# Mamba-2 SSD and an ELU feed-forward on one core: the last pair's second layer by 12-bit words instead of Strassen products

## The chip, the core and the metric

The kernel runs on one core of a Trainium2 chip. Its time is device microseconds of that core for one launch. The engines are named as in the profile: PE is TensorE (matmuls), PEld its weight loads, DVE is VectorE, ACT is ScalarE, POOL is GpSimd, SP is SyncE, which issues most transfers.

## The reference

```python
# x [4, 8, 768, 32], a [4, 8, 768], B and C [4, 8, 768, 16]: a chunked scan
y[:, :, sl] = y_intra + y_inter                      # per batch and head, chunks of 32
state = decay_full * state + sum(Bx)
...
x = y.transpose(0, 2, 1, 3).reshape(3072, 256)       # tokens by (head, dim)
h = x @ w_in                                         # [3072, 256] @ [256, 2048]
g = where(h > 0, h, exp(min(h, 0)) - 1)              # ELU
return g @ w_out                                     # [3072, 2048] @ [2048, 256], float32
```

Inputs and output are float32. The two layers of the feed-forward are the bulk of the work of TensorE.

## The kernel before

**Tiles.** The 3072 tokens are 12 blocks of 256 tokens; two blocks make a pair, named by its first block: n = 0, 2, 4, 6, 8, 10 (`NP` is 12). d_ff = 2048 is 16 blocks of 128, numbered m (`MC` is 16). `g_of[n, m]` holds the ELU output of one m: 128 features by two blocks by 256 tokens.

**Order.** The schedule is written out by hand (`tc.manual_schedule()`): each engine runs its instructions in the order of the source, and waits only by semaphore. From pair 4 on there is one stage per pair n, in the loop `for n in range(4, NP, 2)`: 16 steps k. A step computes one m of the first layer of pair n (`l1_words`), and lets the generator `second(n - 2)` go on by three or four pieces (`l2s`), so that the second layer of the pair before is woven in. In the stages of pairs 4 to 8 the scan of the next pair's tokens is woven in too; in that of pair 10, "the last stage" in the prediction, there is none. After the loop the last pair's second layer runs alone: `second(10, True)`.

**First layer by words** (`l1_words`, L779 to L801). An F32R matmul goes through TensorE in one pass, but keeps fewer bits than float32. So each operand is split into a high and a low word of 12 bits, and a product is three F32R passes: high by high and low by low into the PSUM bank `ps_h`, a pass over the sums into `ps_w`. A step's three passes are six matmuls of 128x512 (L788). Behind them comes a ring over two engines: ACT copies `ps_w` to `e` times 4096 (L796); DVE joins `e` with `ps_h` (L799); ACT makes Relu and Exp (L805, L806, `begin_end`); one step later, ahead of the next L799, DVE makes g from both (L813, `end_words`). For even m POOL then takes a difference inside g (L848, `sub`), which the second layer needs.

**Second layer by Strassen** (`second`, L871 to L960). For a pair, 2x2 blocks of g and of w_out are multiplied with 7 products rather than 8: seven rounds r over a `chunk` of four m-pairs, twice (`half`), with 8 float32 products of 128x128 per round (L907). A float32 product is two matmul records in the trace. The sums of g blocks (`sum_t1`, `sum_t2`, and in-place differences) are made by POOL, sums of weight blocks were made ahead (`a_out`, `s_out`: s1 lies in place in `w_out`), results are added up by DVE (L885 and others) with two copies by ACT.

**PSUM.** `p_a` has seven banks in rotation (tag "a"): `ps_h`, `ps_w` and every second round of `second` take the next one, and wait until the instruction that read its former content is done. `p_o` has one bank; the other rounds take that.

**SBUF.** Tiles come from pools by tag, with `bufs` buffers in rotation. Tag "w64" holds first raw weights, then the weight sums, then `k_words` (words of w_in); "w_in" holds w_in and its low words. By the last stage, the scan's tiles ("bct", "ctm", "xr", "bc", "M", "ec", "b", "L", "yT") are free.

**End.** The last `second` writes its output by four transfers (two of them 64 KB, on ACT's and SP's queues), issued as its parts are complete (L893 to L899, L947).

Of the kernel before, what the change touches and what calls it, by code (L numbers as in the profile page):

```python
# [17 lines left out]
P = 128  # L18
# [14 lines left out]
def kernel(  # L33
# [139 lines left out]
    def w_load(i, parts=1):  # L173
        if i < len(pieces):
            w_raw[i] = conv.tile(
                [P, parts, 2, 2 * CW // parts], U32, tag="w64", name="w64", bufs=W_AHEAD)
# [538 lines left out]
        nc.gpsimd.dma_start(out=out[:, rows], in_=in_[:, rows], accum_op=ALU.add)  # L715

    def weight_sums():
        return [conv.tile([P, MC // 2, P], F32, tag="w64", name="w_sum", bufs=W_AHEAD)
                for _ in range(3)]

    w_parts = w_out.rearrange("p (i k) (r c) -> p k r i c", k=2, c=P)
# [10 lines left out]
    def words_of_w(i):  # L732

        w = pieces[i][0]
        k_words[i] = conv.tile(
            [P, 2, KC, CW], F32R, tag="w64", name="w_words", bufs=W_AHEAD)
        nc.scalar.activation(k_words[i][:, 0], w, ACT.Copy, scale=NEAR)
        nc.vector.scalar_tensor_tensor(
            out=k_words[i][:, 1], in0=k_words[i][:, 0].bitcast(F32), scalar=1.0 / WORD - 1.0,
            in1=w, op0=ALU.mult, op1=ALU.add)  # L740
# [27 lines left out]
    def both_of_y(n):  # L768
# [6 lines left out]
                in1=y[:, k], op0=ALU.mult, op1=ALU.add)  # L775
        y_words[n] = y1, y0, both

    def l1_words(n, m, between=None):

        cols = slice(m % 2 * P, (m % 2 + 1) * P)  # L780
        w, w0 = k_words[m // 2]
        w1, both_w, w0 = w[:, 0, :, cols], w[:, 1, :, cols], w0[:, :, cols]
        y1, y0, both_y = y_words[n]
        high, both = psum([P, 2 * BLK], "ps_h"), psum([P, 2 * BLK], "ps_w")
        passes = [(high, w1, y1), (high, w0, y0), (both, both_w, both_y)]
        for ps, lhs, rhs in passes if m == (8 if n == 2 else 0) or m == 15 else passes[2:] + passes[:2]:
            for k in range(KC):
                nc.tensor.matmul(  # L788
                    out=ps, lhsT=lhs[:, k], rhs=rhs[:, k], start=k == 0 and lhs is not w0,
                    stop=k == KC - 1 and lhs is not w1)  # L790
# [5 lines left out]
        nc.scalar.activation(e, both, ACT.Copy, scale=WORD)  # L796
        if late:
            end_words()
        nc.vector.scalar_tensor_tensor(  # L799
            out=high, in0=high, scalar=WORD - 1.0, in1=e, op0=ALU.mult, op1=ALU.add)  # L800
        late.append((n, m, high, e))  # L801
# [66 lines left out]

    c_of = {}

    def second(n, last=False):  # L871
# [5 lines left out]
        s2, s3, s4 = s_out  # L877
        for half in range(2):
# [3 lines left out]
            chunk = range(4 * half, 4 * half + 4)  # L882

            def add(out, in0, in1, eng=nc.vector):
                eng.tensor_tensor(out=out, in0=in0, in1=in1, op=ALU.add)  # L885

            for r, a in enumerate((a11, a12, s1, s2, s3, a22, s4)):
                if last and half and r == 6:
                    store(n, 0)
                    for ts, queue in enumerate((nc.scalar, nc.sync)):  # L890
                        ps = psum([P, P], "ps_o")
                        for i in chunk:
                            nc.tensor.matmul(  # L893
                                out=ps, lhsT=quarters(n, i)[3][:, ts * P:(ts + 1) * P],
                                rhs=a[:, i], start=(i == chunk[0]), stop=(i == chunk[-1]))
                        nc.vector.tensor_tensor(
                            out=c12[:, ts], in0=ps, in1=c12[:, ts], op=ALU.add)
                        r0 = row_of(n + 1) + ts * P
                        queue.dma_start(out=out[r0:r0 + P, 0:P], in_=c12[:, ts])  # L899
                    return  # L900
                pool, tag = (p_a, "a") if (7 * half + r) % 2 else (p_o, "o")
                ps = pool.tile([P, 2, P], F32, tag=tag, name="ps_o")
                for i in chunk:
                    b11, b21, b12, b22 = quarters(n, i)
                    b = (b11, b21, b12, t2_of[n, i], b11, b21, b22)[r]
                    for ts in range(2):
                        nc.tensor.matmul(  # L907
                            out=ps[:, ts], lhsT=b[:, ts * P:(ts + 1) * P], rhs=a[:, i],
                            start=(i == chunk[0] and ts == 0), stop=(i == chunk[-1]),
                            skip_group_check=True)  # L910
                    if i < chunk[-1]:
                        yield
                if r == 0:
                    if half:
                        add(p5, ps, c22)
                        add(c21, ps, c21)
                        add(c11, ps, c11)
                    else:
                        nc.scalar.copy(out=p1, in_=ps)
                    for i in chunk:  # L920
                        b11 = quarters(n, i)[0]
                        sub(b11, t2_of[n, i], b11)
                elif r == 1:
                    add(c11, ps, c11 if half else p1)
                    for i in chunk:
                        b21 = quarters(n, i)[1]
                        sub(b21, b21, t2_of[n, i])
                elif r == 2:
                    add(p5, ps, p5 if half else p1)
                elif r == 3:  # L930
                    add(p5, ps, p5)
                    if half:
                        add(c12, c12, p5, nc.gpsimd)
                        add(c21, ps, c21)
                    else:
                        add(u, ps, p1)
                elif r == 4:
                    if half:
                        add(c21, ps, c21)
                    else:  # L940
                        add(u, ps, u)
                    add(c22, ps, p5)
                    if not half:
                        nc.scalar.copy(out=c12, in_=ps)  # L944
                    if last and half:
                        r0 = row_of(n + 1)
                        nc.sync.dma_start(  # L947
                            out=out[r0:r0 + BLK, P:2 * P].rearrange("(t p) c -> p t c", p=P),
                            in_=c22)
                    if not half:  # L950
                        sum_t2(n, 1)
                    elif n + 2 < NP:
                        sum_t2(n + 2, 0)
# [6 lines left out]
                yield  # L960

    def store(n, at):
        r0 = row_of(n + at)
# [346 lines left out]
    for n in range(4, NP, 2):  # L1310
# [37 lines left out]
        if m:  # L1348
            l2s(4)
            both_of_y(m)  # L1350
        end_words()
# [37 lines left out]
```

## Time and profile before

| what | us |
|---|---|
| median of the runs | 347.59 |
| lowest run | 346.96 |
| the profiled execution | 347.65 |
| its span, first to last instruction | 345.9 |
| last stage (16 steps), from the span's start | 270.42 to 317.49 |
| last pair's second layer alone | 317.49 to 342.66 |
| drain | 342.66 to 345.90 |

The span is shorter than the time because the launch has work around the first and last instruction. A busy time is a sum over instructions, so a share says how full an engine is, not that it is what the others wait for. Matmuls are pipelined: a record of 275 ns can be followed by the next one 112 ns later, so prices of matmuls are taken from start to start, in the chain of work that ended last. In the rows of groups the numbers are minimum/median/maximum in ns; in the rows of the timeline they are start, duration, engine, line, operation, output<-input, shape, and in brackets the idle time before and what ended it.

### The profile page before, as it was taken

To read this page: it belongs to the slowest core of one execution; us is meant where nothing else is said; L and a number is where in the kernel's file an instruction comes from. 1 tells how busy PE (TensorE), PEld (TensorE's weight loads), DVE (VectorE), ACT (ScalarE), POOL (GpSimd) and SP (SyncE) were. 2 spreads that over 40 slices of the span, in tenths; PEclk is the share of its full clock that TensorE was granted. 3 is DMA by queue.
4 is the path that set the end of the run, shared out by engine and by line. 5 is a ranking of instruction groups with operands and counts; after the bars stand their busy time and mean duration, and the time that the engine had idled before them with its cause. 6 is when DMAs were issued, how large, how long until landed. Compare 5 with 4: busy or idle time off the path is not lost.

```text
span 345.9 us, 9861 instructions
## 1 busy us (share of the span) xinstructions
PE 338.7 (98%) x3878; PEld 297.4 (86%) x3878; DVE 253.3 (73%) x504; ACT 238.1 (69%) x541; POOL 215.3 (62%) x321
## 2 busy tenths in 40 slices
PE   8989999999999999999999999999999999999996
PEld 4669888888788898889899888999988999999996
DVE  4898988879898778866788676878676766665222
ACT  5688989599759898657699457699457566565000
POOL 5553553559989699964396664296754264455760
PEclk9999999999999999999999999999999999999999
DMA  8888988470797961070511170410000100001001
GB/s 145 228 231 165 326 178 236 87 140 30 107 151 112 139 108 31 10 162 2 124 45 32 17 153 5 116 22 3 2 0 4 63 0 3 0 0 63 2 1 62
DMA packets 76902, 28.58 MB, mean 83 GB/s; under 512 B 57848, under 2 KB 71736, under 8 KB 76856
## 3 DMA queue, kind: packets, MB, share of 16 engines
q1 hardware_dynamic: 70360, 25.60, 32.2%
q0 software_dynamic: 4176, 2.10, 5.4%
q8 instruction: 30, 0.49, 0.6%
q10 hardware_dynamic: 2320, 0.26, 0.5%
q14 instruction: 16, 0.13, 0.1%
HBM read 22.51 MB, written 3.34 MB: 75 GB/s over the span
## 4 chain that ended last, share of the span: by engine, by line
PE 92%; SPq 2%; DMA 2%; DVE 1%; ACT 1%; issue 1%; POOL 0%; POOLq 0%; ACTq 0%
PE ps_o L907 36%; PE ps_h L788 19%; PE ps_h L671 11%; PE ps_w L788 10%; PE ps_o L832 8%; PE ps_y L638 3%; DMA w<-in_moe_w_in_dram 2%; PE ps_g L545 2%; PE ps_y L620 2%; PE ps_st L575 1%; SPq L179 1%; PE ps_o L893 1%; SPq L132 0%; POOL w_in L252 0%; SPq L116 0%
## 5 line engine op out<-in xcount | busy, mean ns | idle before, releaser
L907 PEld LDWEIGHTS ps_o<-w_out,g 128*128 128x128 f32 x640 | 78.6, 192 | 3.4
L907 PE MATMUL ps_o<-w_out,g 128*128 128x128 f32 x640 | 80.3, 276 | 0.0
L805 ACT ACTIVATE e<-ps_h 128x512 f32<-128x512 f32 x72 | 43.0, 597 | 50.2 <-DVE ps_h L799 50.1
L813 DVE SCALAR_TENSOR_TENSOR g<-e,ps_h 128x512 f32<-128x512 f32 x72 | 49.4, 686 | 34.1 <-ACT e L806 33.7
L848 POOL TENSOR_TENSOR g<-g 128x256 f32<-128x256 f32 x36 | 28.0, 777 | 56.2 <-DVE g L813 56.0
L799 DVE SCALAR_TENSOR_TENSOR ps_h<-ps_h,e 128x512 f32<-128x512 f32 x72 | 50.1, 695 | 12.5 <-ACT e L796 9.7
L788 PE MATMUL ps_w<-y_both,w_words 128*128 128x512 f32 x144 | 51.1, 435 | 0.0
L796 ACT ACTIVATE e<-ps_w 128x512 f32<-128x512 f32 x72 | 42.2, 587 | 12.9 <-PE ps_w L788 12.8
L671 PE MATMUL ps_h<-yT,w_in 128*128 128x256 f32 (+1 forms) x208 | 45.2, 368 | 2.3 <-POOL w_in L252 2.2
L806 ACT ACTIVATE e<-e 128x512 f32<-128x512 f32 x72 | 45.5, 632 | 2.3
L788 PE MATMUL ps_h<-y,w_words 128*128 128x512 f32 x144 | 46.1, 402 | 0.0
L788 PE MATMUL ps_h<-y,w 128*128 128x512 f32 x144 | 44.7, 392 | 0.0
L671 PEld LDWEIGHTS ps_h<-yT,w_in 128*128 128x128 f32 x208 | 36.4, 190 | 8.3 <-POOL w_in L252 3.7
L525 ACT ACTIVATE L<-L,ncum 128x64 f32<-128x64 f32 x160 | 42.2, 336 | 0.2
L907 PE MATMUL ps_o<-w_sum,g 128*128 128x128 f32 x304 | 38.4, 275 | 0.0
L907 PEld LDWEIGHTS ps_o<-w_sum,g 128*128 128x128 f32 x304 | 37.0, 192 | 1.2 <-ACT c_sum L944 0.2
L530 POOL TENSOR_SCALAR_AFFINE_SELECT L<-L 64x512 f32<-64x512 f32 x40 | 30.0, 749 | 9.1 <-ACT L L525 7.7
L788 PEld LDWEIGHTS ps_h<-y,w 128*128 128x128 f32 x144 | 27.1, 188 | 6.5 <-POOL w L848 0.2
L848 POOL TENSOR_TENSOR g<-t,g 128x256 f32<-128x256 f32 x40 | 28.0, 730 | 5.9 <-PE ps_o L907 5.7
L788 PEld LDWEIGHTS ps_h<-y,w_words 128*128 128x128 f32 x144 | 26.4, 188 | 5.7 <-issue 0.4
L832 PE MATMUL ps_o<-w_out,g 128*128 128x256 f32 x128 | 31.0, 384 | 0.0
L848 POOL TENSOR_TENSOR t<-g 128x256 f32<-128x256 f32 x40 | 28.6, 746 | 0.2
(131 smaller groups left out, 535.1 us busy)
## 6 DMA issues: line engine op xcount, KB each, us to landing
L<-flat SPq DMA_DIRECT2D x20, 256.0 KB
w<-in_moe_w_out_dram SPq DMA_DIRECT2D x8, 512.0 KB
w<-in_moe_w_in_dram SPq DMA_DIRECT2D x7, 512.0 KB
xr<-in_x_dram SPq DMA_DIRECT2D x24, 128.0 KB
out_dram<-c_sum SPq DMA_DIRECT2D x9, 256.0 KB
bc<-in_B_dram SPq DMA_DIRECT2D x24, 64.0 KB
w_sum<-w_out POOLq DMA_DIRECT2D x3, 512.0 KB, 8.9
bc<-in_C_dram SPq DMA_DIRECT2D x22, 64.0 KB
```

The costliest lines, as they stand in the source:

```text
L525: nc.scalar.activation(L[:, h, u], L[:, h, u], ACT.Exp, bias=ncum[:, u, row:row + 1])
L530: nc.gpsimd.affine_select(out=part, in_=part, pattern=[[0, 4], [0, 2], [1, Q]], compare_op=ALU.is_ge, fill=0.0, base=0, channel_multiplier=-1)
L671: nc.tensor.matmul(out=ps[:, j, toks], lhsT=w_in[i][:, k, j * P:(j + 1) * P], rhs=yT[n // 2][:, k, n % 2].rearrange("p u i -> p (u i)")[:, ...
L788: nc.tensor.matmul(out=ps, lhsT=lhs[:, k], rhs=rhs[:, k], start=k == 0 and lhs is not w0, stop=k == KC - 1 and lhs is not w1)
L796: nc.scalar.activation(e, both, ACT.Copy, scale=WORD)
L799: nc.vector.scalar_tensor_tensor(out=high, in0=high, scalar=WORD - 1.0, in1=e, op0=ALU.mult, op1=ALU.add)
L805: nc.scalar.activation(e, high, ACT.Relu, scale=-1.0)
L806: nc.scalar.activation(e, e, ACT.Exp, scale=-1.0)
L813: nc.vector.scalar_tensor_tensor(out=g_of[n, m].rearrange("p b i -> p (b i)"), in0=e, scalar=1.0, in1=h, op0=ALU.subtract, op1=ALU.max)
L832: nc.tensor.matmul(out=o_of[n][:, ts], lhsT=g_of[n, j][:, m % 2, ts * P:(ts + 1) * P], rhs=w_out[:, m], start=(m == 0 and ts == 0), stop=( ...
L848: nc.gpsimd.tensor_tensor(out=out, in0=in0, in1=in1, op=ALU.subtract)
L907: nc.tensor.matmul(out=ps[:, ts], lhsT=b[:, ts * P:(ts + 1) * P], rhs=a[:, i], start=(i == chunk[0] and ts == 0), stop=(i == chunk[-1]), s ...
```

## The change

The last pair's second layer is made by words too, as in the first layer: each g and each w_out block is split in three (a high word, a sum word for the pass over sums, a low word), and each product of 128 tokens by 128 features by 256 columns is three F32R matmuls. There are four output tiles of 128 tokens, 16 m and three kinds: 192 matmuls of 128x256. Kind 1 goes to the second half of a tile's bank, kinds 0 and 2 to the first; ACT copies the one and DVE joins both at the end. Three tiles lie in `p_a`, the fourth in `p_o`.

The words are spread: in the last stage ACT makes high words of g (`high_of_g`) in steps 2, 3, 4, 6, 8, 12 and 14 and high words of w_out (`high_of_out`) in steps 5, 7, 9 and 11; DVE makes the other words of g (`rest_of_g`) and the sum word of w_out, POOL its low word (`rest_of_out`), a step later. The others follow in `second_words`, in 14 groups, up to seven groups ahead of their matmuls. POOL restores the weight block that held a sum (`given_back`) in steps 4 and 12. Words of w_out lie in the scan's free tiles (`HOMES`), words of g in the free buffers of "w64" and "w_in".

The order of m is exchanged for pairs 8 and 10: 8 to 15, then 0 to 7. `second(8)` accordingly begins with the second half. For pair 10 the differences that POOL made in g for Strassen are gone (the condition `n + 2 < NP`), and so are the last pair's sums. The buffers of "w64" are split into 8 and 3 ("s64"), by which every tile keeps the place in rotation that it had. `end_words` for the last m moves from the loop's end to the second group of the new part. In the last two m the four tiles are finished one after the other, each with its ACT copy, its DVE join and a transfer of 128 KB from SP.

```diff
+    def ends_of(n):
+        return (8, 7) if n >= NP - 4 else (8, 15) if n == 2 else (0, 15)
...
-        if m % 2 == 0 and (n, m) != (2, 14):
+        if m % 2 == 0 and (n, m) != (2, 14) and n + 2 < NP:
             sub(g_of[n, m][:, 1], g_of[n, m][:, 1], g_of[n, m][:, 0])
...
+    def given_back(rows):
+        sub(a_out[2][:, rows], a_out[2][:, rows], a_out[3][:, rows])
...
+    def high_of_out(at):
...
+        for part, rows in parts_of(v[0], p):
+            nc.scalar.activation(part, w_out[:, rows], ACT.Copy, scale=NEAR)
...
+    def rest_of_out(at):
...
+        for part, rows in parts_of(v_of[p][1], p):
...
+            nc.vector.scalar_tensor_tensor(
+                out=part, in0=high.bitcast(F32), scalar=1.0 / WORD - 1.0, in1=w_out[:, rows],
+                op0=ALU.mult, op1=ALU.add)
+        for part, rows in parts_of(v_of[p][2], p):
...
+            sub(part, w_out[:, rows], high.bitcast(F32))
...
+    def high_of_g(n, m):
...
+        nc.scalar.activation(tiles[0], g_of[n, m], ACT.Copy, scale=NEAR / WORD)
...
+    def rest_of_g(n, m, which=(1, 2)):
+        for k in which:
+            nc.vector.scalar_tensor_tensor(
+                out=h_of[m][k], in0=h_of[m][0].bitcast(F32), scalar=(1.0 - WORD, WORD)[k - 1],
+                in1=g_of[n, m], op0=ALU.mult, op1=(ALU.add, ALU.subtract)[k - 1])
...
+    def second_words(n):
+        ps = [psum([P, 2, DM], "ps_o") for _ in range(3)]
+        ps.append(p_o.tile([P, 2, DM], F32, tag="o", name="ps_o"))
...
+        for at, m in enumerate(TURN[:-2]):
+            if at + 7 < MC:
+                high_of_g(n, TURN[at + 7])
+            if at + 6 < MC:
+                rest_of_g(n, TURN[at + 6])
+            if at == 1:
+                end_words()
+            if at in (0, 2, 4, 6):
+                high_of_out(4 + at // 2)
+            if at in (1, 3, 5, 7):
+                rest_of_out(4 + at // 2)
+            for t in range(4):
+                for kind in (1, 0, 2):
+                    product(m, t, kind)
+        for t in range(4):
+            for m in TURN[-2:]:
+                product(m, t, 1)
+            o = ffn.tile([P, DM], F32, tag="t2", name="o", bufs=4)
+            nc.scalar.activation(o, ps[t][:, 1], ACT.Copy, scale=WORD)
+            for m in TURN[-2:]:
+                product(m, t, 0)
+                product(m, t, 2)
+            nc.vector.scalar_tensor_tensor(
+                out=o, in0=ps[t][:, 0], scalar=WORD - 1.0, in1=o, op0=ALU.mult, op1=ALU.add)
+            r0 = row_of(n + t // 2) + t % 2 * P
+            nc.sync.dma_start(out=out[r0:r0 + P, :], in_=o)
...
-            l1_words(n, k, between=m if k == 15 else None)
+            l1_words(n, (k + 8) % MC if n >= NP - 4 else k, between=m if k == 15 else None)
...
             if not m:
                 l2s(4 if k % 2 else 3)
+                if k in (4, 12):
+                    given_back(slice(4, 8) if k == 4 else slice(0, 4))
+                if k in (5, 7, 9, 11):
+                    high_of_out(k // 2 - 2)
+                if k in (6, 8, 10, 12):
+                    rest_of_out(k // 2 - 3)
+                if k in (2, 3, 4, 6, 8, 12, 14):
+                    high_of_g(n, TURN[(2, 3, 4, 6, 8, 12, 14).index(k)])
+                if k == 3:
+                    rest_of_g(n, TURN[0])
+                if 4 <= k < 12:
+                    rest_of_g(n, TURN[k // 2 - 1], (1 + k % 2,))
+                if k in (13, 15):
+                    rest_of_g(n, TURN[5], (k // 2 - 5,))
                 continue
...
-    n = NP - 2
-    for k, _ in enumerate(second(n, True)):
-        if k == 0:
-            store(n - 2, 0)
-            store(n - 2, 1)
+    second_words(NP - 2)
```

More of the change, by code (lines that the diff above doesn't have):

```diff
@@ L175, in w_load @@
             w_raw[i] = conv.tile(
-                [P, parts, 2, 2 * CW // parts], U32, tag="w64", name="w64", bufs=W_AHEAD)
+                [P, parts, 2, 2 * CW // parts], U32, tag="s64" if 5 <= i < 8 else "w64", name="w64",
+                bufs=3 if 5 <= i < 8 else W_AHEAD - 3)
             for part in range(parts):
@@ L717, in weight_sums @@
     def weight_sums():
-        return [conv.tile([P, MC // 2, P], F32, tag="w64", name="w_sum", bufs=W_AHEAD)
+        return [conv.tile([P, MC // 2, P], F32, tag="s64", name="w_sum", bufs=3)
                 for _ in range(3)]
@@ L735, in words_of_w @@
         k_words[i] = conv.tile(
-            [P, 2, KC, CW], F32R, tag="w64", name="w_words", bufs=W_AHEAD)
+            [P, 2, KC, CW], F32R, tag="w64", name="w_words", bufs=W_AHEAD - 3)
         nc.scalar.activation(k_words[i][:, 0], w, ACT.Copy, scale=NEAR)
@@ L785, in l1_words @@
         passes = [(high, w1, y1), (high, w0, y0), (both, both_w, both_y)]
-        for ps, lhs, rhs in passes if m == (8 if n == 2 else 0) or m == 15 else passes[2:] + passes[:2]:
+        for ps, lhs, rhs in passes if m in ends_of(n) else passes[2:] + passes[:2]:
             for k in range(KC):
@@ L869, with second @@
     c_of = {}
-    def second(n, last=False):
+    def second(n):
         c = c_of[n] = ffn.tile([P, 2, 2, 2, P], F32, tag="c", name="c_sum", bufs=1)
@@ L877, in second @@
         s2, s3, s4 = s_out
+        turns = (1, 0) if n == NP - 4 else (0, 1)
         for half in range(2):
@@ L881, in second @@
                 p1, p5, u = (tmp[:, r] for r in range(3))
-            chunk = range(4 * half, 4 * half + 4)
+            chunk = range(4 * turns[half], 4 * turns[half] + 4)
             def add(out, in0, in1, eng=nc.vector):
@@ L887, in second @@
             for r, a in enumerate((a11, a12, s1, s2, s3, a22, s4)):
[L888 to L900, printed above, removed]
                 pool, tag = (p_a, "a") if (7 * half + r) % 2 else (p_o, "o")
@@ L944, in second @@
                         nc.scalar.copy(out=c12, in_=ps)
[L945 to L949, printed above, removed]
                     if not half:
-                        sum_t2(n, 1)
-                    elif n + 2 < NP:
-                        sum_t2(n + 2, 0)
+                        sum_t2(n, turns[1])
+                    elif n + 4 < NP:
+                        sum_t2(n + 2, int(n + 2 == NP - 4))
                 elif r == 5:
@@ L960, in second, with rooms @@
                 yield
+    v_of, h_of = {}, {}
+    def given_back(rows):
+        sub(a_out[2][:, rows], a_out[2][:, rows], a_out[3][:, rows])
+    def rooms(tag, count):
+        pool, bufs, shape = {
+            "bct": (att, 2, [P, 2, DM]), "ctm": (att, 2, [P, 2, DM]), "xr": (raw, 3, [P, 2, DM]),
+            "bc": (raw, 2, [P, 2, DM]), "M": (att, 8, [P, 1, DM]), "ec": (att, 4, [P, 1, DM]),
+            "b": (raw, 2, [P, 1, DM]), "L": (att, 2, [P, 2, 2, DM]), "yT": (ffn, 2, [P, 2, 2, DM])}[tag]
+        tiles = [pool.tile(shape, F32R, tag=tag, name="v", bufs=bufs) for _ in range(count)]
+        return [t[:, k] for t in tiles for k in range(2)] if len(shape) == 4 else tiles
@@ new lines @@
+    HOMES = [(("bct", 2), ("ctm", 1)), (("ctm", 1), ("xr", 2)), (("xr", 1), ("bc", 2)), (("M", 6),),
+             (("M", 2), ("ec", 4)), (("L", 2),), (("yT", 1),), (("yT", 1), ("b", 2))]
+    def high_of_out(at):
+        p = (at + 4) % 8
+        tiles = [t for tag, count in HOMES[at] for t in rooms(tag, count)]
+        if at == 5:
+            spare.append(tiles.pop())
+        if at == 6:
+            tiles.append(spare.pop())
+        v = [tiles[:2], tiles[2:4], tiles[4:]] if len(tiles) == 6 else [[tiles[0]], [tiles[1]], tiles[2:]]
+        v_of[p] = v
+        for part, rows in parts_of(v[0], p):
+            nc.scalar.activation(part, w_out[:, rows], ACT.Copy, scale=NEAR)
@@ new lines, in parts_of, with out_words @@
+    def parts_of(tiles, p):
+        count = 2 // len(tiles)
+        return [(t, slice(2 * p + at * count, 2 * p + (at + 1) * count)) for at, t in enumerate(tiles)]
+    def out_words(p, kind, m):
+        tiles = v_of[p][kind]
+        return tiles[0][:, m % 2] if len(tiles) == 1 else tiles[m % 2][:, 0]
+    def rest_of_out(at):
+        p = (at + 4) % 8
+        v1 = v_of[p][0]
+        for part, rows in parts_of(v_of[p][1], p):
+            high = v1[0] if len(v1) == 1 else v1[rows.start % 2]
+            nc.vector.scalar_tensor_tensor(
+                out=part, in0=high.bitcast(F32), scalar=1.0 / WORD - 1.0, in1=w_out[:, rows],
+                op0=ALU.mult, op1=ALU.add)
+        for part, rows in parts_of(v_of[p][2], p):
+            high = v1[rows.start % 2 if len(v1) == 2 else 0]
+            if len(v1) == 1 and len(v_of[p][2]) == 2:
+                high = high[:, rows.start % 2:rows.start % 2 + 1]
+            sub(part, w_out[:, rows], high.bitcast(F32))
@@ new lines @@
+    spare = []
+    TURN = [(m + 8) % MC for m in range(MC)]
+    def high_of_g(n, m):
+        if m == TURN[1]:
+            both = ffn.tile([P, 2, 2, BLK], F32R, tag="yT", name="g_words")
+        else:
+            both = conv.tile([P, 2, 2, BLK], F32R, tag="w64", name="g_words", bufs=W_AHEAD - 3)
+        tiles = [both[:, 0], both[:, 1], conv.tile(
+            [P, 2, BLK], F32R, tag="w_in", name="g_words", bufs=DF // CW + 1)]
+        h_of[m] = tiles
+        nc.scalar.activation(tiles[0], g_of[n, m], ACT.Copy, scale=NEAR / WORD)
@@ new lines, in rest_of_g, with product @@
+    def rest_of_g(n, m, which=(1, 2)):
[6 more added lines that the diff above has]
+        ps.append(p_o.tile([P, 2, DM], F32, tag="o", name="ps_o"))
+        def product(m, t, kind):
+            lhs = h_of[m][kind][:, t // 2, t % 2 * P:(t % 2 + 1) * P]
+            nc.tensor.matmul(
+                out=ps[t][:, int(kind == 1)], lhsT=lhs, rhs=out_words(m // 2, kind, m),
+                start=(m == TURN[0] and kind == 1), stop=(m == TURN[-1] and kind > 0),
+                skip_group_check=True)
+        store(n - 2, 0)
+        store(n - 2, 1)
+        for at, m in enumerate(TURN[:-2]):
[24 more added lines that the diff above has]
+            nc.sync.dma_start(out=out[r0:r0 + P, :], in_=o)
@@ L1350 @@
             both_of_y(m)
-        end_words()
+        if m:
+            end_words()
         for _ in steps:
             pass
-    n = NP - 2
-    for k, _ in enumerate(second(n, True)):
-        if k == 0:
-            store(n - 2, 0)
-            store(n - 2, 1)
+    second_words(NP - 2)
 _INS = ['x', 'a', 'B', 'C', 'moe_w_in', 'moe_w_out']
```

## The prediction

> **What bounds the kernel now.** I read the page's busy line first, then the table of busy time by stretch for the end of the run, then the chain of work that ended last for the same stretch. After that I read rows of single engines for the prices.
>
> ```profile
> PE 338.7 (98%) x3878; PEld 297.4 (86%) x3878; DVE 253.3 (73%) x504; ACT 238.1 (69%) x541; POOL 215.3 (62%) x321
> ```
>
> ```profile
> core 0: us, PE busy (x) PEld busy (x) DVE busy (x) ACT busy (x) POOL busy (x), PEclk, DMA share, GB/s
> 270.42:317.49 47.07, 47.07 (x324) 43.14 (x322) 29.86 (x53) 28.58 (x51) 23.07 (x33) 1.00 0.06 18
> 317.49:342.66 25.17, 25.17 (x226) 24.98 (x224) 8.49 (x21) 1.75 (x4) 14.51 (x21) 1.00 0.07 22
> 342.66:345.90 3.24, 0.01 (x1) 0.00 (x0) 0.29 (x1) 0.00 (x0) 0.00 (x0) 0.92 0.26 81
> ```
>
> ```profile
> 313.94 0.56 PE ps_o L907 x5
> 314.49 0.92 PE ps_h L788 x4
> 315.42 0.45 PE ps_w L788 x2
> 315.87 25.01 PE ps_o L907 x224
> ```
>
> TensorE is the bound throughout. The three stretches are the last stage (the first layer of pair 10 mixed with the second layer of pair 8), the last pair's own second layer, and the drain. TensorE never idles in the first two, and its clock is 1.00. In the middle stretch ACT does 1.75 us and DVE 8.49 us of 25.17: these are the engines that the change loads. The profiled execution took 347.65 us, 1.75 more than its span of 345.9, and is 0.06 above the median of 347.59. I sum against 347.65.
>
> **Matmul price.** The change drops 112 float32 products, which the trace records as 224 matmuls, and adds 192 matmuls of one pass, 128x256, each with its own weights. Removed: 224 x 0.1117 (25.01/224) = 25.0 us. The trace has no one-pass matmul of 256 columns. The one-pass 128x512 costs 0.92/4 to 0.45/2 = 0.228; half is 0.114. The bounds: 0.1117, the short float32 record, since that has the same weights to load; and 0.123, if what a one-pass 512 costs above a 128x256 float32 record (0.216 in the chain: "PE ps_h L671 x8" 1.73) is a fixed 0.012 on top of 0.1117. I take 0.114, nearest in kind: 192 x 0.114 = 21.9, bounds 21.4 to 23.6. **TensorE: -3.1 us** (-3.6 to -1.4), if it never waits.
>
> **What is added on ACT and DVE in the last stage.** ACT gets 7 conversions of g, 3 of weights and two halves. DVE gets 12 + 3 of 128x512 and two halves. POOL loses 8 differences of 0.73 (5.8) and gets two of 128x512 that undo a weight sum, and four parts of weight words; one 128x512 on POOL is 1.27 (line L252). That is 23.07 - 5.8 + 2.5 + 5.3 = 25.0 us, 53% of the stage.
>
> These lie on a ring that runs once a step: ACT copies ps_w (L796), DVE joins it with ps_h (L799), ACT twice (L805, L806), DVE makes g (L813).
>
> ```profile
> 272.08 0.60 ACT L796 ACTIVATE e<-ps_w 128x512 f32<-128x512 f32 x1 [0.93 <-PE ps_w L788]
> 273.44 0.60 ACT L805 ACTIVATE e<-ps_h 128x512 f32<-128x512 f32 x1 [0.77 <-DVE ps_h L799]
> 274.07 0.63 ACT L806 ACTIVATE e<-e 128x512 f32<-128x512 f32 x1
> ```
>
> ```profile
> 308.74 0.63 ACT L806 ACTIVATE e<-e 128x512 f32<-128x512 f32 x1
> 309.28 0.58 ACT L796 ACTIVATE e<-ps_w 128x512 f32<-128x512 f32 x1
> ```
>
> From these starts a round is 2.53: 1.36 from L796 to L805, 0.63, 0.54. TensorE's step is 47.07/16 = 2.94, so the ring has 0.41 to spare. One conversion of 0.6 on ACT makes it 3.13: 0.19 lost per step. Steps 2 to 9 have one each (1.5), step 5 also a copy of 0.37, and the later steps about balance: the ring ends some 2 us behind TensorE, which banks of PSUM can hide. The third output tile of the new last stage takes the bank that L813 of step 14 empties; that ended at 315.98, and TensorE would want the bank at 317.49 + 6 x 0.114 = 318.17. **A lag of 2.2 us is free**; it would just fit.
>
> **The port.** All added DVE instructions but the last four read two operands from SBUF. L799 and L813 read one, the other is PSUM. The rows of the same form in the trace:
>
> ```profile
> L738 DVE SCALAR_TENSOR_TENSOR w_words<-w_words,w_in x8: 683/910/2377, 79.3 to 117.8; 128x512 fp32r<-128x512 f32 x8
> ```
>
> ```profile
> 106.52 2.38 DVE L738 SCALAR_TENSOR_TENSOR w_words<-w_words,w_in 128x512 fp32r<-128x512 f32 x1
> 106.53 1.81 POOL L848 TENSOR_TENSOR w<-w_in,w_words 128x256 fp32r<-128x256 f32 x2
> ```
>
> ```profile
> 81.02 1.86 POOL L848 TENSOR_TENSOR w<-w_in,w_words 128x256 fp32r<-128x256 f32 x2
> 81.41 2.01 DVE L773 SCALAR_TENSOR_TENSOR y_both<-y,yT 128x512 fp32r<-128x512 f32 x2
> ```
>
> L738 takes 0.683 at best and up to 2.377, the long ones beside POOL arithmetic; at 81 us two on each engine take turns, 2.4 us for all four. Alone, such DVE instructions start 0.60 apart (L773 at 270.09, two in 1.29). So DVE's conversions and POOL's instructions add up in time.
>
> In the stage, 17 conversions meet a busy POOL 53% of the time and wait about half an instruction, 0.4: 17 x 0.21 = 3.6 us. About half lands on the ring, because DVE's work behind L799 (0.61 + 0.36 + 0.60, at times a second conversion) about fills the 2.02 (0.73 + 0.63 + 0.66) before L813 may start: 1.8. Lag 2.0 + 1.8 = 3.8, less the free 2.2: **+1.6 us**. Bounds 0 (no wait lands) and 3.5 (all do, 3.6 + 2.0 - 2.2).
>
> **The new last stage.** TensorE starts at 317.5 + 1.6 = 319.1. DVE is through L799 of step 15 (316.54 in the trace, + 3.8), an add and the last conversion of the loop at 321.9. It then has 20 conversions x 0.60, one L813 (0.69) and 3 x 0.60 + 2 x 0.36 of weight words: 15.2 us. POOL has its last thirds of weight words here, four of 0.70 (t<-g at 310.85, four in 2.81) and two of 1.27 = 5.3, less 0.69 beside L813, which doesn't need the port: 4.6. The first words of the last block are the last conversion but one: 321.9 + 15.2 + 4.6 - 0.6 = 341.1. TensorE comes to them after 169 matmuls, at 319.1 + 19.3 = 338.4: **+2.7 us** of waiting. Bounds: 0 if POOL fits elsewhere (then 336.5, in time); 4.5 with conversions of 0.69 (20 x 0.09 more). ACT's 13 conversions of 0.6 run ahead.
>
> **Drain.** The last join is 128x256 (0.42, as L885) in place of 128x128 (0.29): +0.1, and one 128 KB transfer in place of 64 KB, hidden in the same landing time. Edits at nothing: the buffer split hands every tile the buffer it had; the exchanged order at pairs 8 and 10 moves equal steps about; storing pair 8 is issued by SP while TensorE works.
>
> **Sum:** 347.65 - 3.1 + 1.6 + 2.7 + 0.1 = 348.95, say **349.0 us**: no change that this kernel's measurement tells apart (about 2%, 7 us).
>
> The Trainium skill, SBUF — State Buffer, "Who interferes with whom", says that a DVE instruction with two SBUF inputs and a GpSimd one that reads SBUF exclude each other, whoever starts first holding the port for its whole length. The row at 106.52 waited 1.7 us, longer than one POOL instruction of the pair beside it, so here the trace is harsher than one blocked instruction; by the rule alone the sum is the 349.0 above, by that row it goes to 352.
>
> **Rivals.** (1) *The cover holds.* If conversions slip between POOL's instructions, lag stays at 2.0 and the last words come at 336.5 to 338: 347.65 - 3.1 + 0.1 + 0.1 = 344.8. For it: DVE's share stays near 80%, POOL's subtractions come in strings with gaps. Against: the rows at 81 and 106. (2) *Weights set the pace*, the other side. If a one-pass matmul must wait for its own load, 0.19 us in the trace (L907 PEld, mean 192 ns), 192 x 0.19 = 36.5: 347.65 + 11.5 + 1.6 + 0.1 = 360.9. It loses from 25.0/192 = 0.130 on. Against: the float32 records come every 0.112 with loads of 0.192. In the Trainium skill, TensorE: Matmul & The Clock Gate, "Part 3: Packing small matmuls", it says that a load overlaps running matmuls only where the row groups differ; that would be this rival, and the 0.112 pitch disagrees. (3) *DVE loses the port again and again*, as at 106.52: 0.5 us more on eight conversions: 353.
>
> **How the numbers follow.** Port conflict as summed, 347 to 352.5: 0.68. Cover holds, 344 to 347: 0.18. DVE loses repeatedly, 352.5 to 355: 0.07. Weights set the pace: 0.05. Better than all, down to 340: 0.02. The range 345.0 to 352.5 takes the first case and the upper half of the second, 0.8. The likeliest one's own is 347 to 352.5. Faster by over 2% (under 340.6): 0.01. Slower (over 354.5): 0.05 and a little of (3), 0.07. Within: 0.92.
>
> **What would show it.** Right: matmuls into ps_o 0.114 apart where nothing waits; conversions (L1019, L993) with a median over 0.7 and several above 1.2 beside POOL; TensorE waiting on DVE at the start of the last stage and for the last blocks' words. Wrong: conversions all near 0.69 and no idle TensorE (rival 1); a pitch of 0.19 (rival 2); an idle TensorE released by ACT, which would mean that I mis-sized the ring.

## The result, and the profile after

The changed kernel took 352.0 us (median), the one before 347.54 in the same comparison: ratio 1.0132, 95% interval 1.0104 to 1.0159. One of the six runs of the kernel before took 480.62 us; the ratio leaves it out. The changed kernel is slower by 1.3%, inside the predicted range of 345.0 to 352.5 and 3 us above the predicted 349.0. The profiled execution took 351.88 us with a span of 350.2, that is 4.3 us more span than before.

The busy line, and busy time by stretch: the last stage, the new second layer by itself, the drain.

```profile
PE 339.7 (97%) x3846; PEld 296.1 (85%) x3846; DVE 278.4 (80%) x530; ACT 250.9 (72%) x569; POOL 210.9 (60%) x301
```

```profile
270.47:318.79 48.32, 47.20 (x322) 42.92 (x320) 40.96 (x67) 31.36 (x58) 25.55 (x28) 1.00 0.04 12
318.79:346.65 27.86, 25.21 (x195) 23.54 (x193) 22.55 (x33) 11.78 (x24) 7.46 (x6) 1.00 0.09 30
346.65:350.20 3.55, 0.00 (x1) 0.00 (x0) 0.42 (x1) 0.00 (x0) 0.00 (x0) 0.61 0.21 70
```

The columns are those of the same table in the prediction. The stage grew from 47.07 to 48.32, the part behind it from 25.17 to 27.86, the drain from 3.24 to 3.55. TensorE now idles in both of the first two; DVE went from 29.86 to 40.96 busy us in the one and from 8.49 to 22.55 in the other. The chain of work that ended last used to be TensorE alone. For the part behind the loop it now reads:

```profile
321.69 3.56 DVE g_words L1019 x5
325.25 0.60 DVE g L817
325.84 1.78 DVE v L993 x2
327.62 4.60 DVE g_words L1019 x4
332.22 0.60 DVE v L993
332.82 2.41 DVE g_words L1019 x4
335.23 0.60 DVE v L993
335.83 2.41 DVE g_words L1019 x4
338.24 0.60 DVE v L993
338.84 1.82 DVE g_words L1019 x3
...
340.71 0.40 PE ps_o L1030
341.11 0.02 issue
341.13 0.39 ACT o L1055
341.52 0.04 issue
341.56 0.99 PE ps_o L1030 x6
342.56 0.02 issue
342.58 0.39 ACT o L1055
```

Up to 340.7 it is DVE's conversions one after the other, the groups beside POOL's work stretched (four conversions in 4.60, later four in 2.41). After that TensorE and ACT alternate, once per output tile. Inside the stage too a conversion is stretched beside POOL; alone it takes 0.68:

```profile
305.04 1.74 POOL L852 TENSOR_TENSOR v<-w_out,v 128x512 fp32r<-128x512 f32 x1
305.56 1.78 DVE L1019 SCALAR_TENSOR_TENSOR g_words<-g_words,g 128x512 fp32r<-128x512 f32 x1
```

TensorE's own timeline has the gaps, the first in the stage and the others at the end; in brackets is the idle time and what ended it:

```profile
312.46 0.68 PE L899 MATMUL ps_o<-w_out,g 128*128 128x128 f32 x4 [1.12 <-DVE c_sum L890]
```

```profile
340.71 0.39 PE L1030 MATMUL ps_o<-v,g_words 128*128 128x256 f32 x1 [0.54 <-DVE g_words L1019]
341.56 0.98 PE L1030 MATMUL ps_o<-v,g_words 128*128 128x256 f32 x6 [0.47 <-ACT o L1055]
343.02 0.97 PE L1030 MATMUL ps_o<-v,g_words 128*128 128x256 f32 x6 [0.47 <-ACT o L1055]
344.46 0.97 PE L1030 MATMUL ps_o<-v,g_words 128*128 128x256 f32 x6 [0.47 <-ACT o L1055]
345.91 0.74 PE L1030 MATMUL ps_o<-v,g_words 128*128 128x256 f32 x4 [0.47 <-ACT o L1055]
```

The bracket counts only the time in which no record runs. From start to start the four stops are 0.86, 0.75, 0.75 and 0.75 us where 0.12 is normal, and the matmul after each start comes 0.22 later: 3.05 us of excess over 0.12 for ACT. The excess before that, waiting for words, is 1.6 us in all.

| term (span against span) | predicted | measured |
|---|---|---|
| last stage (ring and port) | +1.6 | +1.3 |
| 192 matmuls for 224 | -3.1 | -2.0 |
| waits for words | +2.7 | +1.6 |
| waits for ACT at the tiles' ends | none | +3.05 |
| drain | +0.1 | +0.3 |
| sum | +1.3 | +4.3 |

The second row is what the part behind the loop grew by, 2.69, less the two rows of waits. The matmuls come 0.117 to 0.120 apart where nothing waits.

### The profile page after: what moved, and what is told of

The parts are those of the page before. It is cut to its first block, busy times and chain, and to the rows that moved or that the text cites. A ratio compares the mean times of both kernels' runs of the same rounds, so it can differ in the third digit from the quotient of the medians.

```text
span 350.2 us, 9808 instructions
## 1 busy us (share of the span) xinstructions
PE 339.7 (97%) x3846; PEld 296.1 (85%) x3846; DVE 278.4 (80%) x530; ACT 250.9 (72%) x569; POOL 210.9 (60%) x301
## 4 chain that ended last, share of the span: by engine, by line
PE 75%; DVE 11%; ACT 5%; issue 3%; SPq 2%; DMA 2%; POOL 0%; DVEq 0%; ACTq 0%; POOLq 0%
PE ps_o L899 24%; PE ps_h L792 16%; PE ps_h L672 11%; PE ps_w L792 8%; PE ps_o L836 8%; DVE g_words L1019 5%; PE ps_y L639 3%; DVE ps_h L803 2%; DMA w<-in_moe_w_in_dram 2%; DVE v L993 2%; PE ps_g L546 2%; PE ps_y L621 2%; ACT e L809 1%; PE ps_st L576 1%; PE ps_o L1030 1%
## 5 line engine op out<-in xcount | busy, mean ns | idle before, releaser
L817 DVE SCALAR_TENSOR_TENSOR g<-e,ps_h 128x512 f32<-128x512 f32 x72 | 49.2, 684 | 29.9 <-ACT e L810 29.4
L899 PEld LDWEIGHTS ps_o<-w_out,g 128*128 128x128 f32 x512 | 64.0, 191 | 4.7 <-issue 1.3
L899 PE MATMUL ps_o<-w_out,g 128*128 128x128 f32 x512 | 65.4, 275 | 1.1 <-DVE c_sum L890 1.1
L852 POOL TENSOR_TENSOR g<-g 128x256 f32<-128x256 f32 x28 | 22.2, 792 | 35.6 <-DVE g L817 35.3
L899 PE MATMUL ps_o<-w_sum,g 128*128 128x128 f32 x256 | 32.5, 275 | 0.0
L899 PEld LDWEIGHTS ps_o<-w_sum,g 128*128 128x128 f32 x256 | 31.4, 192 | 1.2 <-ACT c_sum L936 0.2
L1030 PE MATMUL ps_o<-v,g_words 128*128 128x256 f32 x192 | 25.2, 287 | 2.7 <-ACT o L1055 1.9
L836 PEld LDWEIGHTS ps_o<-w_out,g 128*128 128x128 f32 x128 | 23.7, 190 | 3.9 <-ACT ob L842 0.4
```

Of the source, the lines that this page charges most:

```text
L817: nc.vector.scalar_tensor_tensor(out=g_of[n, m].rearrange("p b i -> p (b i)"), in0=e, scalar=1.0, in1=h, op0=ALU.subtract, op1=ALU.max)
L836: nc.tensor.matmul(out=o_of[n][:, ts], lhsT=g_of[n, j][:, m % 2, ts * P:(ts + 1) * P], rhs=w_out[:, m], start=(m == 0 and ts == 0), stop=( ...
L899: nc.tensor.matmul(out=ps[:, ts], lhsT=b[:, ts * P:(ts + 1) * P], rhs=a[:, i], start=(i == chunk[0] and ts == 0), stop=(i == chunk[-1]), s ...
L1030: nc.tensor.matmul(out=ps[t][:, int(kind == 1)], lhsT=lhs, rhs=out_words(m // 2, kind, m), start=(m == TURN[0] and kind == 1), stop=(m == ...
```

## Experiments

Theory: POOL's subtractions and DVE's two-operand conversions exclude each other, and TensorE is held by DVE's words and, at the end, by ACT's copies. Rival: DVE and ACT are late by the sum of their own work. The kernels start from the changed one. Each ratio is to the kernel before, measured along with it. A difference of two ratios is uncertain by about 1 us, as their intervals say, so the traces are read beside it.

**e1: tile ends in another order** (ratio 1.0041, 1.0020 to 1.0061; 349.65 us).

```diff
+        os = []
         for t in range(4):
             for m in TURN[-2:]:
                 product(m, t, 1)
             o = ffn.tile([P, DM], F32, tag="t2", name="o", bufs=4)
             nc.scalar.activation(o, ps[t][:, 1], ACT.Copy, scale=WORD)
+            os.append(o)
+        for t, o in enumerate(os):
             for m in TURN[-2:]:
                 product(m, t, 0)
...
```

> The last two blocks' sum-word matmuls are issued for all four output tiles first, then the other two kinds tile by tile. Theory (TensorE stands still at each tile's end because the next matmul into that bank is held until ACT has copied the bank's second half; four gaps of 0.75 to 0.86 us where 0.12 would do, and a second one of 0.22 each, about 3.0 us): 352.0 falls by 2.3 to 3.2, to about 349.2, and the rows 'PE ps_o <- ACT o' leave the waits. Rival (the gaps only fill time in which the last words or the transfers would hold the end anyway): less than 0.7 us gained.

TensorE's timeline now has one run to the end, after the same wait for DVE:

```profile
340.44 3.03 PE L1030 MATMUL ps_o<-v,g_words 128*128 128x256 f32 x23 [0.53 <-DVE g_words L1019]
```

The ratio fell by 0.9%, 3.2 us; in the traces the part behind the loop fell from 27.86 to 24.96. That is the whole excess within the uncertainty, so nothing else stood behind it. The wait is written in the program: the next matmul into a tile's bank waits until ACT's copy from that bank has been done, though the two touch different halves. No run leaves that wait out. With six or more other matmuls in between (0.72 us and more), the copy of 0.38 is over in time.

**e2: DVE makes the last low words** (1.0068, 1.0043 to 1.0092; 350.52 us). **e3: no subtraction there at all**, the low words are left out (1.0066, 1.0042 to 1.0090; 350.4 us). For the four weight pairs behind the loop:

```diff
-            sub(part, w_out[:, rows], high.bitcast(F32))
+            if at < 4:
+                sub(part, w_out[:, rows], high.bitcast(F32))
+            else:          # e2; in e3: nc.scalar.activation(part, w_out[:, rows], ACT.Copy, scale=NEAR)
+                nc.vector.tensor_tensor(
+                    out=part, in0=w_out[:, rows], in1=high.bitcast(F32), op=ALU.subtract)
```

> In the part after the loop DVE makes the low words of w_out itself (2.4 to 2.8 us more work on DVE), POOL makes none there. Port theory (a DVE instruction with two SBUF operands and a POOL subtraction take turns, so POOL's 5 to 7 us there are added to DVE's): DVE's conversions there are all 0.67 to 0.70, the last words come 2 to 3 us earlier, TensorE's 1.7 us of waiting for words goes, 352.0 falls by 1.2 to 1.8. Rival (DVE is simply late by its own work): DVE has more to do, the last words come 2 to 3 us later, 354 to 355.

> In the part after the loop ACT writes a plain copy of w_out in place of the low words (the difference is left out), POOL does nothing there and DVE what it did. Port theory: DVE's conversions are all 0.67 to 0.70 and 4 to 6 us are gained on DVE, but TensorE can gain only the 1.7 us that it waited for words: 350.2 to 350.8. Rival (DVE late by its own work): unchanged, 351.6 to 352.4.

In e2 DVE has more to do and the kernel is faster, by 2.2 us by the ratios (0.64%) and by 1.3 in the traces (the part behind the loop takes 26.56 us, not 27.86). The start of the new part in e2 and e3, first rows of TensorE's timeline; up to the first tile end no matmul in them starts more than 0.4 us after the one before:

```profile
318.91 21.00 PE L1034 MATMUL ps_o<-v,g_words 128*128 128x256 f32 x170
340.38 0.98 PE L1034 MATMUL ps_o<-v,g_words 128*128 128x256 f32 x6 [0.47 <-ACT o L1059]
```

```profile
318.91 20.64 PE L1033 MATMUL ps_o<-v,g_words 128*128 128x256 f32 x170
340.02 0.97 PE L1033 MATMUL ps_o<-v,g_words 128*128 128x256 f32 x6 [0.47 <-ACT o L1058]
```

So POOL's subtractions cost DVE more than doing them itself would: in the changed kernel the conversions behind the loop took 3.9 us longer in sum than alone, and the subtractions take DVE about 2.5. The difference is about the 1.3 gained. The rival falls.

**e7: e1 and e2 together** (1.0002, 0.9987 to 1.0017; 348.02 us).

> Both the new order of the tile ends and DVE's own low words. If the two costs are separate, the gains add: 352.0 - 3.0 - 1.6 = 347.4 (346.8 to 348.2), level with the kernel before. If the second only hides behind the first: no better than the better one alone, about 349.

The ratio falls by 0.0130, against 0.0091 and 0.0064 for the single edits: most of both, and the same within the uncertainty. It is level with the kernel before, as far as this measurement goes.

**e4 and e5: eight more POOL instructions** that read SBUF, or that only write it.

```diff
+        scr = conv.tile([P, KC, 2 * BLK], F32, tag="y1", name="scratch", bufs=1)
         for at, m in enumerate(TURN[:-2]):
+            if 2 <= at < 10:
+                sub(scr[:, 0, 0:DM], w_out[:, 15], w_out[:, 14])   # e5: nc.gpsimd.memset(scr[:, 0, 0:DM], 0.0)
```

> Eight more POOL subtractions of 128x256 from SBUF to a scratch tile, in groups 2 to 9 of the part after the loop, beside DVE's conversions; nothing waits for them. Port theory: each holds up DVE by about 0.6 us and DVE's last words are what TensorE waits for: 352.0 rises by 3.5 to 5.0, with more conversions above 1.2 us. Rival (POOL and DVE don't disturb each other): no change within 0.5 us.

> Eight more POOL instructions at the same places that only write the scratch tile (a fill of 128x256, no operand is read). If the shared thing is a read path of DVE's second operand: no change, 351.5 to 352.5. If any POOL instruction holds DVE up: plus 1.5 to 4 us, by POOL's time for a fill.

e4: 355.62 us, ratio 1.0232 (1.0210 to 1.0253), 3.5 us above the changed kernel. e5: 351.62 us, 1.0117 (1.0102 to 1.0132), no change from the changed kernel that can be told. The conversions' rows, e4 first, then e5, then the changed kernel (minimum/median/maximum, first and last start):

```profile
L1019 DVE SCALAR_TENSOR_TENSOR g_words<-g_words,g x32: 675/716/1775, 281.8 to 344.7; 128x512 fp32r<-128x512 f32 x32
```

```profile
L1019 DVE SCALAR_TENSOR_TENSOR g_words<-g_words,g x32: 675/682/1783, 281.6 to 340.3; 128x512 fp32r<-128x512 f32 x32
```

```profile
L1019 DVE SCALAR_TENSOR_TENSOR g_words<-g_words,g x32: 674/680/1780, 281.9 to 340.6; 128x512 fp32r<-128x512 f32 x32
```

The last conversion starts 4.1 us later where POOL reads, about 0.5 per POOL instruction, and at the same time where it only writes; in e5 conversions beside a fill took 0.68, as alone. That is the Trainium skill's rule (SBUF — State Buffer, "Who interferes with whom"): two SBUF inputs on DVE contend with a GpSimd instruction that reads SBUF, not with one that only writes it. Both halves of it hold here.

**e6: half as wide, twice as many matmuls** (one run, 371.1 us).

```diff
-            nc.tensor.matmul(
-                out=ps[t][:, int(kind == 1)], lhsT=lhs, rhs=out_words(m // 2, kind, m),
+            for c in range(2):
+                cols = slice(c * P, c * P + P)
+                nc.tensor.matmul(
+                    out=ps[t][:, int(kind == 1), cols], lhsT=lhs,
+                    rhs=out_words(m // 2, kind, m)[:, cols],
...
```

> Each of the 192 matmuls of 256 columns is two of 128, with the same weights loaded again. What sets the 0.117 to 0.120 us from one to the next? If it is columns plus a fixed 0.013: about 0.067 for each of 384, 25.6 us in all, some 2.7 us more. If it is the weight load: 0.107 to 0.12 for each of 384, 41 to 46 us in all, 18 to 23 us more, and DVE's words no longer hold anything up.

```profile
318.20 38.16 PE L1032 MATMUL ps_o<-v,g_words 128*128 128x128 f32 x340
```

38.16/340 = 0.112 us each for 128 columns, against 0.120 for 256. So with 128 the columns don't set the pace, and with 256 it is hardly above that floor. What the two kinds have in common is a weight load of 128x128 each, and that the load sets the floor is the likeliest reading; e6 doesn't part it from another cost of every matmul. A fixed price of any matmul it is not: in the kernel before, 54 small ones with loads of 64x32 (L638) took 0.81 us in the chain, 0.015 each. So halving the price of the 512-column matmul (0.114) came near only because it lay close to a floor. A load's record is 0.19 us long, so at 0.112 the loads do overlap other work of TensorE; the rival in which they don't (0.19 each) is out.

**e8 to e12: the last stage.** All on top of e7. e8 replaces POOL's low words inside the stage by `nc.gpsimd.memset(part.bitcast(F32), 0.0)`. e9 gives them to DVE and undoes the weight sum in step 14 in place of 12. e10 does only the latter:

```diff
-                if k in (4, 12):
+                if k in (4, 14):
                     given_back(slice(4, 8) if k == 4 else slice(0, 4))
```

> On top of the kernel with both edits (348.0): POOL's four low words of w_out inside the last stage are fills with zero, which read nothing (these low words are left out of the product). Port theory: the long conversion of step 10 (1.78 us at 305.6) falls to about 0.7, the ring is 1 us earlier at step 12, and TensorE's stop of 1.1 us there falls below 0.5: 347.2 to 347.6. Rival (the stop comes from ACT's conversions on the ring alone): the stop stays 1.0 to 1.2, 347.8 to 348.3.

> On top of the kernel with both edits: the low words inside the last stage go to DVE too, and the weight sum is undone in step 14 rather than 12. DVE gets 2.5 us more work in the stage and loses about 3 us of waiting. If the waits were on the ring: 347.0 to 347.6, ahead of the kernel before by a little. If DVE's own time is what counts there: 348 to 349.

> On top of the kernel with both edits: only the weight sum is undone in step 14 rather than 12, where DVE has no conversion. The pair of weight conversions in step 12 (2.27 us) falls to about 1.3, DVE begins the part after the loop up to 1 us earlier and the last words are no longer waited for (0.3 us); the stop in step 13 lies ahead of it and stays: 347.5 to 348.0.

e8: 346.6 us, 0.9969 (0.9953 to 0.9986). e9: 348.91, 1.0033 (1.0020 to 1.0046). e10: 347.8, 0.9998 (0.9987 to 1.0010). In e8 TensorE has no stop in the stage. In e7 there was one of 1.10, and these are the conversions of steps 9 and 10, in e7 and then in e8:

```profile
302.38 1.10 DVE L1023 SCALAR_TENSOR_TENSOR g_words<-g_words,g 128x512 fp32r<-128x512 f32 x1
304.94 1.08 DVE L993 SCALAR_TENSOR_TENSOR v<-v,w_out 128x512 fp32r<-128x512 f32 x1
305.94 1.77 DVE L1023 SCALAR_TENSOR_TENSOR g_words<-g_words,g 128x512 fp32r<-128x512 f32 x1
```

```profile
301.53 1.22 DVE L1023 SCALAR_TENSOR_TENSOR g_words<-g_words,g 128x512 fp32r<-128x512 f32 x1
304.20 0.67 DVE L993 SCALAR_TENSOR_TENSOR v<-v,w_out 128x512 fp32r<-128x512 f32 x1
304.80 0.68 DVE L1023 SCALAR_TENSOR_TENSOR g_words<-g_words,g 128x512 fp32r<-128x512 f32 x1
```

The 1.77 met POOL's 128x512 subtraction (305.44 to 307.17 in e7). In e8 there is none, and the fill in its place is over at 302.66. The conversion of step 9, beside POOL's string of four, stays long in both. e8 gained 1.2 us over e7 by the ratios, more than the 0.4 to 0.8 expected. e9 shows the other side: inside the stage DVE has no time to give. Its stops are at 306.28 (0.94), 313.07 (0.20) and at the last words (0.76), and the kernel is slower than e7. In e10 the pair of step 12 fell from 2.27 to 1.72, less than expected, and the median moved by no more than the measurement's spread; the last words are no longer waited for, and the stop stayed, at 1.12.

**e11 and e12: the port kept free by timing.** Both start from e10. The words of the third weight pair, POOL's subtraction with them, are made a step or two later, where POOL was idle (e11); then the conversion of step 9 is moved away from POOL's strings (e12).

```diff
-                if k in (5, 7, 9, 11):
-                    high_of_out(k // 2 - 2)
-                if k in (6, 8, 10, 12):
-                    rest_of_out(k // 2 - 3)
+                if k in (5, 7, 10, 11):
+                    high_of_out((5, 7, 10, 11).index(k))
+                if k in (6, 8, 11, 12):
+                    rest_of_out((6, 8, 11, 12).index(k))
...
-                if 4 <= k < 12:
+                if 4 <= k < 9:                  # from here on e12
                     rest_of_g(n, TURN[k // 2 - 1], (1 + k % 2,))
+                if k == 10:
+                    rest_of_g(n, TURN[3], (2,))
+                if k in (11, 13):
+                    rest_of_g(n, TURN[4], (k // 2 - 4,))
```

> On top of the kernel with both edits and the later undoing: the words of the third weight pair are made a step or two later (ACT in step 10 for 9, DVE and POOL in step 11 for 10), when POOL has no other work, so that POOL's 128x512 subtraction no longer meets the conversion of step 10. Port theory: the 1.77 us conversion falls to 0.7 to 1.0, TensorE's stop in step 13 from 1.1 to 0.2 to 0.6 us: 347.0 to 347.5, a little below the kernel before. If only the sum of work on the ring counts: 347.8 again.

> On top of the last one: no conversion of g in step 9, beside POOL's strings of four; the three that stood in steps 9 to 11 stand in 10, 11 and 13. If the waits of 1.1 to 1.2 us beside the strings were on the ring too: another 0.3 to 0.8 us, 346.5 to 347.2. If DVE then meets the same strings in step 10 and has too much in step 13: 347.2 to 348.2.

e11: 346.08 us, 0.9963 (0.9950 to 0.9976). e12: 345.71 us, 0.9948 (0.9935 to 0.9962), about 1.8 us under the kernel before and 6 under the changed one. The longest conversion and the whole second layer of e12:

```profile
L1023 DVE SCALAR_TENSOR_TENSOR g_words<-g_words,g x32: 675/684/1340, 282.0 to 337.4; 128x512 fp32r<-128x512 f32 x32
```

```profile
317.28 23.28 PE L1034 MATMUL ps_o<-v,g_words 128*128 128x256 f32 x192
```

The 192 matmuls run through in 23.28 us with no stop, and TensorE has none in the stage either; the same two things hold of e11. e11 gained somewhat more than its range said (346.08 against 347.0 to 347.5), and e12 came out below its own (345.71 against 346.5 to 347.2). That e12 is better than e11 isn't shown: their intervals overlap, and in e12 one conversion still takes 1.23 beside POOL. The order of work inside one stage is worth as much as the change of method: the matmuls' own gain is 25.0 - 23.0 = 2.0 us, and e12 keeps about that.

## Why the prediction was right, and where it was off

**The sign and the mechanism.** The forecast was a small loss, because DVE's added conversions share a path with POOL. That was right, and shown: e5 against e4, e2 and e3 behind the loop, e8 inside it. The size was not: 4.5 us between the medians where 1.35 was forecast, and the interval tells the loss from none, which the prediction thought this measurement would not do. The four terms of the sum came to +1.2 together where +1.3 was forecast, because their errors cancel, and a fifth term of 3.05 was missing. That 352.0 still lies in the range is partly luck: the room above 349.0 had been left for more waits on the port.

**"+1.6 us" in the stage** measured 1.3, but not where it was expected. The prediction lets the third tile take the bank that the L813 of step 14 empties. In the program it takes the one that the L813 of step 13 empties. That line is L817 now; these are its rows for steps 13 and 14:

```profile
317.04 0.69 DVE L817 SCALAR_TENSOR_TENSOR g<-e,ps_h 128x512 f32<-128x512 f32 x1
319.66 0.69 DVE L817 SCALAR_TENSOR_TENSOR g<-e,ps_h 128x512 f32<-128x512 f32 x1 [1.00 <-ACT e L810]
```

TensorE began the third tile at 319.59 without a wait, before the second of them. So the free 2.2 us was taken from the wrong instruction; the excess at the start of the part is 0.08 us. The lag was paid earlier, as the stop of 1.12 in the one-bank pool `p_o`, for DVE's addition, which the prediction didn't consider. That its term came close is luck. The conversions of the stage took 5.4 us longer in sum than alone, where 3.6 was summed, and TensorE stopped for 1.1.

**"+2.7 us" for the last words** measured 1.6, in seven small stops and one of 0.7. Most of the difference is the mis-sized pitch of the matmuls (below): at 0.120 TensorE comes to the last words 169 x 0.006 = 1.0 us later, and waits as much less. It also set out 0.3 us earlier than summed, and DVE made the words 0.4 earlier (340.66 for 341.1): it began 0.3 later, but POOL cost it 3.9 us and not 4.6.

**"192 x 0.114 = 21.9"** is mis-sized: 0.120, 23.0 us. I halved the 512-column row. The bound of 0.123 held it, and e6 shows that it sits near a floor of 0.112 that half the columns pay too.

**"ACT's 13 conversions of 0.6 run ahead" and the drain's +0.1** left out what costs most: in the tile ends ACT's copy stands between two matmuls of the same tile. Each tile's second half is complete, ACT copies it (0.38), and only then may TensorE go on into the first half; 3.05 us. This step was missing from the sum, not mis-sized. The diff showed the order, and the program's list of waits names ACT ahead of each of these matmuls. I had costed the copy as an instruction that nobody waits for. With it and the measured pitch, which adds 1.1 to the matmuls and takes 1.0 from the waits, the sum would have been 349.0 + 3.05 + 0.1 = about 352.2, against 351.88 for the profiled execution. The drain's other 0.2 is not explained by a run.

**What I said would show it.** Waits on DVE: yes for the last words, no at the start of the part. Matmuls 0.114 apart: no, 0.120. Conversions above 1.2 us beside POOL: yes. A median over 0.7: no, 0.680 for L1019; most conversions met no POOL work, and a few long ones carry the cost. An idle TensorE released by ACT was named as a sign of a mis-sized ring. It came, at the tile ends, and meant something else: the copies that were not in the sum. Rival 1 (cover holds, 344.8) is about what e12 reaches, after the cover was made. Rival 2 is out by e6. Rival 3 would have given 353, near the measured time, by 4 us more of waiting in the conversions. They waited 9.3 us in all where 8.2 was summed, so it is not what happened.

What stays open: why a conversion beside POOL waits for one POOL instruction in some places and longer in others. No run was made for it.

## What to carry to other kernels

Before moving work to an engine that looks idle, look at which operands its instructions read: two from SBUF on DVE added up with POOL's reads here, and it can be cheaper to give the slower engine's part to the busy one, or to shift it by a step. At the end of an accumulation, ask of every matmul which reader of its tile it is held by: a copy of 0.38 us between two matmuls of one tile cost 0.75 us per tile, and other tiles' matmuls in between cost nothing. Price a narrow matmul by a short one that has weights of its own (0.112 us here), not by its share of a wide one. When the price of one engine goes up, redo the waits: a later TensorE waits less for the same words.

## What the runs showed of the hardware

With 128 columns a one-pass matmul comes every 0.112 us, with 256 every 0.120, with 512 every 0.228. The Trainium skill, TensorE: Matmul & The Clock Gate, "LDWEIGHTS (loading the stationary operand)", gives columns / 1.2 GHz, an estimate of 0.107 for 128 columns; the measured floor is near it. At half the clock (below) the 128-column matmuls of e6 came 0.213 apart, so the floor goes with the clock and is not a fixed time.

In e4 TensorE's clock fell to half after it had been busy for only part of a few microseconds:

```profile
333.00:336.00 3.00, 1.15 (x8) 0.74 (x6) 3.00 (x4) 0.00 (x0) 2.92 (x4) 1.00 0.00 0
336.00:340.00 4.00, 3.82 (x19) 3.85 (x20) 4.00 (x5) 0.00 (x0) 3.92 (x4) 0.57 0.00 0
```

The columns are as above; the granted clock is the third from the end. TensorE was busy for 1.15 of 3.00 us, with starts 1.6 and 1.0 us apart, and then matmuls of 256 columns came 0.213 apart, where 0.120 is normal, for some 3.4 us. It cost e4 nothing: the chain that ended last goes through DVE's conversions up to 344.8, and TensorE, slow or not, stood still for words again at 340.6, 341.3 and 344.9.

In e6 it did cost time. From 361.3 on its last matmuls of 128 columns came 0.213 apart instead of 0.112, some 15 x 0.10 = 1.5 us, behind the stops at its tile ends; the row shown of e6 lies ahead of that. Stops of the same length didn't bring it about in the changed kernel's profiled execution, whose clock stayed at 1.00 up to its last matmul. So these traces show that a stopping TensorE can lose half its clock, but not after how much of a stop.
